# Attention stage of a fused attention, MLP and expert kernel: row sums kept in two DRAM rows, two small PSUM uses moved into the output's banks, scores issued in another order

## The chip, the cores and the metric

The kernel runs on one core of one Trainium2 chip. The metric is device microseconds (us) of one execution; lower is better. Engines are written as in the profile: PE (TensorE, with PEld for its weight loads), DVE (VectorE), ACT (ScalarE), POOL (GpSimd) and SP (SyncE, which here only issues DMAs; "SPq" in the rows). Each engine takes its instructions in order.

## The reference

Block-causal softmax attention, then a leaky MLP, then eight experts mixed by a Sinkhorn-normalised gate. Only the first of the three matters here:

```python
# q, k, v: (4 batches, 8 heads, 576 positions, 64 features), float32
scores = scale * np.matmul(q, k.transpose(0, 1, 3, 2))
scores = np.where(block_i >= block_j, scores, -1000000000.0)   # blocks of 64 positions: 9 x 9
scores = scores - np.max(scores, axis=-1, keepdims=True)
attn = np.exp(scores)
attn = attn / (np.sum(attn, axis=-1, keepdims=True) + 1e-09)
x = np.matmul(attn, v)          # -> (2304 tokens, 512) for the MLP
x = leaky(x @ w_in) @ w_out     # the MLP: 512 -> 2048 -> 512
out = sum_e P[:, e] * (relu(x @ w1[e]) @ w2[e])   # 8 experts, P from 8 rounds of row and column normalisation
```

## The kernel before

The attention works on 16 *pairs*: two heads of one batch, one head on partitions 0 to 63 and one on 64 to 127. A pair's 576 positions are 9 blocks of 64 queries (`NQ = 9`). For a pair p:

- `load_qk` and `load_v` issue its loads on SP: two for q, one for the 64-position tails of q, the same for k, and four for v. `turn_q`, `turn_k` and `turn_tail` transpose q, k and the two tails on PE into a PSUM tile of the pool `ps_tr` (two tiles in turn); ACT copies q out with the scale (`spread`), DVE copies k (`place_k`).
- `scores(p, i, ...)` multiplies query block i with the keys up to it, takes the negated maximum on DVE (`nmax`) and the exponential with its sum on ACT (`ex`, `ssum`). For odd blocks the two heads are written crosswise (`crossed`), so their transposition by `swap` puts them right again.
- `turn_attn(p, g)`, g = 0 to 6, transposes the 25 squares of the exponentials on PE, four at a time (the last one alone), and ACT (g even) or DVE (g odd) copies them into `at`.
- `weigh` multiplies `at` with v into the PSUM tile `av` of the pool `ps_av` (two banks, one tile): `first_product` is the first key chunk, `other_parts` are six products of the other three chunks.
- `totals(p)` forms the reciprocal of the sums, `rsum` (128 partitions x 9), and writes it to a DRAM row of 2 x 576 numbers: one DMA for the five straight (even) blocks of both heads, and one each for the four crossed blocks of either head. `spread_totals(p)` reads that row back with two DMAs, each of which puts one head's 576 numbers on 64 partitions (`by_feature`).
- `split_x(p)` multiplies `av` by `by_feature` on DVE (`xs`) and splits the result into two parts for the MLP (ACT, POOL).

The loop over p overlaps four pairs. The list `turns` sets the order on PE by hand (PE is in `manual_schedule`); "prv", "cur", "nxt" and "fol" in it are the pairs p - 1, p, p + 1 and p + 2. So in *period* p, PE does the scores of pair p + 1, the transpositions and first product of pair p, the other products of pair p - 1 and the turns of pair p + 2. `totals(p)` stands at the period's head, and `load_qk(p + 3)` behind its end. The order on the other engines comes from the framework's scheduler. On SP a period is: three writes of the row, four loads of v, two reads of the row, six loads of q, tails and k; in eight periods a 512 KB load of MLP weights (`wraw`) stands somewhere between. A read of the row waits on SP for the row's writes, and everything behind it on SP waits with it.

Once the attention is done, the MLP and the experts run to the end on PE.

Of the kernel before, what the change touches and what calls it, by code (L numbers as in the profile page):

```python
# [8 lines left out]
F32 = mybir.dt.float32  # L9
# [3 lines left out]
ALU = mybir.AluOpType  # L13
AX = mybir.AxisListType

P = 128
BLK = 64
# [10 lines left out]
def f32(ap):  # L28
    return ap.bitcast(F32)
# [7 lines left out]
def block_attention_mlp_moe(  # L37
# [15 lines left out]
    nc = tc.nc  # L53
    B, H, S, D = q.shape
# [3 lines left out]
    NQ = S // BLK  # L58
# [23 lines left out]
    dram = ctx.enter_context(tc.tile_pool(name="dram", bufs=2, space=bass.MemoryType.DRAM))  # L82
# [10 lines left out]
    def x_parts(c, t0, t1):  # L93

        if t0 < XCUT:
            return [t[:, c, t0:t1] for t in x_first]
        return [t[:, c, t0 - XCUT:t1 - XCUT] for t in x_late]
# [117 lines left out]
    def attention(att, ps_sc, ps_tr, ps_av):  # L215
# [14 lines left out]
        nmax = [att.tile([P, NQ + 1], F32, name=f"nmax{i}") for i in range(2)]  # L230
        ssum = [att.tile([P, NQ + 1], F32, name=f"ssum{i}") for i in range(2)]
        rsum = [att.tile([P, NQ], F32, name=f"rsum{i}") for i in range(2)]
        by_feature = [att.tile([P, S], F32, name=f"by_feature{i}") for i in range(2)]
        xs = att.tile([P, S], F32, name="xs")
        order = [(i, c) for c in range(NKC) for i in range(2 * c, NQ)]
        base = [order.index((2 * c, c)) for c in range(NKC)]
# [38 lines left out]
        def spread(p, src, lo, n):  # L275
            scale = 1.0 / float(D) ** 0.5
            nc.scalar.activation(
                out=qT[p % 2][:, lo * BLK:(lo + n) * BLK], in_=src[:, 0:n * BLK], func=AF.Copy, scale=scale
            )

        def place_k(p, src, lo, hi):
            nc.vector.tensor_copy(out=kT[p % 2][:, lo:hi], in_=src)

        def turn_q(p):
            qm = ps_tr.tile([P, 512], F32, name="qm", tag="tr")
            for t in range(NFULL):
                nc.tensor.transpose(qm[:, t * P:(t + 1) * P], qraw[:, t, :], ident)
            spread(p, qm, 0, W // BLK)
# [5 lines left out]
            place_k(p, km[:, 0:W], 0, W)  # L294

        def turn_tail(p):
            tail = ps_tr.tile([P, 512], F32, name="qk_tail", tag="tr")
            nc.tensor.transpose(tail[:, 0:2 * TAIL], tails, ident)
            spread(p, tail, W // BLK, TAIL // BLK)
            place_k(p, tail[:, TAIL:2 * TAIL], W, S)  # L300
# [41 lines left out]
        rows = {}  # L342

        def totals(p):
            r, s = rsum[p % 2], ssum[p % 2][:, 0:NQ]
            nc.gpsimd.tensor_scalar(out=r, in0=s, scalar1=EPS, scalar2=None, op0=ALU.add)
            nc.vector.reciprocal(out=r, in_=r)
            rows[p] = dram.tile([2, BLK * NQ], F32, name="row", tag="row")
            to = rows[p].rearrange("h (q i) -> h q i", i=NQ)
            nc.sync.dma_start(  # L350
                out=rows[p].rearrange("h (q i) -> (h q) i", i=NQ)[:, 0:NQ:2], in_=r[:, 0:NQ:2]
            )
            for h in range(2):
                nc.sync.dma_start(out=to[1 - h, :, 1:NQ:2], in_=r[h * BLK:(h + 1) * BLK, 1:NQ:2])

        def spread_totals(p):
            with ExitStack() as queued:
                queued.enter_context(tc.issue_after(getattr(fetched[0], "ins", fetched[0])))
                for h in range(2):
                    nc.sync.dma_start(  # L360
                        out=by_feature[p % 2][h * D:(h + 1) * D, :], in_=rows[p][h:h + 1, :].to_broadcast([D, S])
                    )

        def turn_attn(p, g):
            todo = order[4 * g:4 * g + 4]
            n = len(todo)
            tr = ps_tr.tile([P, 4, 2, BLK], F32, name="tr", tag="tr")
            for s, (i, c) in enumerate(todo):
                nc.tensor.transpose(  # L369
                    tr[:, s].rearrange("p h q -> p (h q)"),  # L370
                    ex[p % 2][:, off[i] + c * P:off[i] + (c + 1) * P],
                    swap if i in crossed else ident,
                )
            dst = at[:, 4 * g:4 * g + n]
            if g % 2 == 0:
                nc.scalar.copy(out=dst, in_=tr[:, 0:n])
            else:
                nc.vector.tensor_copy(out=dst, in_=tr[:, 0:n])

        av = {}  # L380

        o = 512 - P

        def weigh(p, c, h, part):
            if (c, h, part) == (0, 0, 0):
                av[p] = ps_av.tile([P, 1024], F32, name="av", tag="av")
            a = at[:, base[c]:base[c] + NQ - 2 * c, h, :]
            r = slice(h * D, (h + 1) * D)
            lhsT = vraw[p % 2][:, c, r]
            if part == 0:  # L390
                nc.tensor.matmul(av[p][r, o:512], lhsT, a[:, 0:2, :], start=True, stop=True)
            else:
                q0 = 2 if c == 0 else 0
                nc.tensor.matmul(  # L394
                    av[p][r, 512 + P * max(c - 1, 0):512 + S - P], lhsT, a[:, q0:, :],
                    start=c == 0, stop=c == NKC - 1,
                )

        def split_x(p):
            b, hp = divmod(p, NPAIR)  # L400
            t = av.pop(p)
            nc.vector.tensor_tensor(  # L402
                out=xs.rearrange("p (i q) -> p i q", q=BLK), in0=t[:, o:o + S].rearrange("p (i q) -> p i q", q=BLK),
                in1=by_feature[p % 2].rearrange("p (q i) -> p i q", i=NQ), op=ALU.mult,
            )
            t0, t1 = b * S, (b + 1) * S
            cuts = [t0, XCUT, t1] if t0 < XCUT < t1 else [t0, t1]
            for u0, u1 in zip(cuts, cuts[1:]):
                hi, lo = x_parts(hp, u0, u1)
                y = xs[:, u0 - t0:u1 - t0]  # L410
                nc.scalar.copy(out=hi, in_=y)
                nc.gpsimd.tensor_tensor(out=lo, in0=y, in1=f32(hi), op=ALU.subtract)
# [3 lines left out]


        first_part = [(weigh, 0, h, part) for part in range(2) for h in range(2)]
        other_parts = [("prv", weigh, c, h, 1) for c in range(1, NKC) for h in range(2)]
        def first_product(p):  # L420
            for f, *a in first_part:
                f(p, *a)

        turns = [
            ("nxt", scores, 8), *other_parts, ("prv", split_x),
            ("nxt", scores, 7, 6), ("cur", turn_attn, 0), ("nxt", load_v), ("fol", turn_q),
            ("nxt", scores, 1, 0), ("cur", turn_attn, 1), ("cur", turn_attn, 2),
            ("nxt", scores, 5, 4), ("fol", turn_tail), ("cur", first_product),
            ("nxt", scores, 3, 2), ("cur", turn_attn, 3), ("fol", turn_k), ("cur", turn_attn, 4),
            ("cur", spread_totals), ("cur", turn_attn, 5), ("cur", turn_attn, 6),  # L430
        ]
        opening = [
            ("nxt", scores, 1, 0), ("nxt", scores, 3, 2), ("nxt", scores, 5, 4), ("nxt", scores, 8),
            ("fol", turn_q), ("nxt", scores, 7, 6), ("nxt", load_v), ("fol", turn_k), ("fol", turn_tail),
        ]

# [11 lines left out]
        for t in vraw:  # L448
            nc.gpsimd.tensor_copy(out=t[TAIL:, NFULL, :], in_=nought[TAIL:, :])
        turn_q(0)  # L450
        turn_k(0)
        turn_tail(0)
        warm(ps_sc, "sc", 3)
        load_qk(1)
# [3 lines left out]
        for p in range(-1, NP + 1):  # L458
            who = {"prv": p - 1, "cur": p, "nxt": p + 1, "fol": p + 2}
            if 0 <= p < NP:  # L460
                totals(p)
            if p == NP:
                first_product(p - 1)
            for w, f, *a in (turns if p >= 0 else opening):
                if 0 <= who[w] < NP and (f is not first_product or p < NP - 1):
                    f(who[w], *a)
                if f is scores and p >= 0 and steps:
                    with ExitStack() as queued:
                        if p + 1 < NP:
                            queued.enter_context(tc.issue_after(getattr(latest[0], "ins", latest[0])))  # L470
                        steps.pop(0)()
            if p + 3 < NP:
                load_qk(p + 3)
# [50 lines left out]
    with (  # L524
        tc.tile_pool(name="att", bufs=1) as att,
        tc.tile_pool(name="ps_sc", bufs=4, space=bass.MemoryType.PSUM) as ps_sc,
        tc.tile_pool(name="ps_tr", bufs=2, space=bass.MemoryType.PSUM) as ps_tr,
        tc.tile_pool(name="ps_av", bufs=1, space=bass.MemoryType.PSUM) as ps_av,
    ):
        with tc.manual_schedule(engines={mybir.EngineType.PE}):  # L530
            attention(att, ps_sc, ps_tr, ps_av)
# [299 lines left out]
    bank, part, hq = {}, {}, {}  # L831
# [377 lines left out]
    for n in range(0, NGR, 2):  # L1209
        p, e, i = groups[n]  # L1210
# [135 lines left out]
```

## Time and profile before

| | us |
|---|---|
| median of 3 runs (2122.15 to 2124.04) | 2122.96 |
| the profiled execution's own time | 2127.02 |
| its span, first to last instruction | 2125.2 |
| PE busy in the span | 2064.7 (97%) |
| DVE / ACT / POOL busy | 1566.6 / 818.6 / 653.7 |
| mean granted TensorE clock | 0.989 |
| first matmul of the MLP starts, from the span's start | 259.0 |
| first write of a row of sums, last one | 17.69, 260.01 |

The attention is the first eighth of the span. In the page's 40 slices of 53 us, PE stands at 7 or 8 tenths in the first five and at 9 (90% or more) in nearly all others. The line numbers below are those of the kernel before: L320 scores, L326 maxima, L333 exponentials, L369 transpositions of the exponentials, L376 and L378 their copies, L391 and L394 products with v, L402 `xs`, L350 and L354 the writes of the row, L360 its reads, L261, L265, L245 and L249 the loads.

### The profile page before, as it was taken

Reading aid. Unit: us, or ns where it says so; the run is one execution under the profiler, and the core shown is the slowest. Engines: PE = TensorE matmul, PEld = TensorE weight load, DVE = VectorE, ACT = ScalarE, POOL = GpSimd, SP = SyncE. Lnnn points to the kernel's source line nnn. Section 1 sums busy time; section 2 is a strip of 40 time slices with the busy share of each in tenths; the row PEclk is TensorE's granted clock in tenths of the full one; section 3 lists DMA queues with packets and bytes.
Section 4 is the critical chain, followed back from the end, with each engine's and each line's share of the span. In section 5 each row is a group of like instructions: output and inputs, shape, how many; then the busy total and the mean of one; then the engine's idle time right before and its main releaser. Section 6 shows DMA issues by size and latency. Waiting matters only on the chain.

```text
span 2125.2 us, 32293 instructions
## 1 busy us (share of the span) xinstructions
PE 2064.7 (97%) x11498; PEld 1853.2 (87%) x11498; DVE 1566.6 (74%) x2671; ACT 818.6 (39%) x1795; POOL 653.7 (31%) x639
## 2 busy tenths in 40 slices
PE   7877799999999999999999999999999999999999
PEld 4444479898888889898989999999999999999998
DVE  6665565656555887887787688888888688888886
ACT  5555433222233454454444333332233423332322
POOL 1121122212202445544543223333232322333322
PEclk9999999999999999999999999999999999999999
DMA  5344311111005888888989777777777777777773
GB/s 116 78 91 97 73 36 50 40 41 50 30 10 189 317 284 310 305 291 297 324 303 339 279 251 262 268 257 265 259 247 274 265 251 252 256 275 254 270 254 111
DMA packets 252642, 436.92 MB, mean 206 GB/s; under 512 B 94761, under 2 KB 131625, under 8 KB 252225
## 3 DMA queue, kind: packets, MB, share of 16 engines
q1 hardware_dynamic: 251280, 434.56, 60.2%
q8 instruction: 91, 1.49, 0.3%
q14 instruction: 71, 0.57, 0.1%
q10 hardware_dynamic: 1200, 0.30, 0.1%
HBM read 308.82 MB, written 125.95 MB: 205 GB/s over the span
## 4 chain that ended last, share of the span: by engine, by line
PE 88%; DMA 6%; DVE 3%; ACT 1%; POOL 1%; SPq 1%; issue 1%; DVEq 0%; ACTq 0%; POOLq 0%
PE h_ps L841 28%; PE o L1009 21%; PE o L1065 12%; PE h_ps L500 9%; PE o L520 9%; DMA row<-rsum 3%; PE o L841 3%; PE sc L320 1%; DMA by_feature<-row 1%; PE tr L369 1%; PE av L394 1%; DMA kraw<-in_k_dram 1%; DVE xs L402 0%; DVE nmax L326 0%; DMA k_0h<-th 0%
## 5 line engine op out<-in xcount | busy, mean ns | idle before, releaser
L938 DVE TENSOR_TENSOR xa<-o,xa 128x384 f32<-128x384 f32 x392 | 216.4, 553 | 111.1 <-PE o L1009 106.9
L841 PE MATMUL h_ps<-xhS,w1h 128*128 128x384 f32 x768 | 257.5, 335 | 0.0
L841 PE MATMUL h_ps<-xhS,w1l 128*128 128x384 f32 x768 | 256.6, 334 | 0.0
L841 PE MATMUL h_ps<-xlS,w1h 128*128 128x384 f32 x768 | 256.6, 334 | 0.0
L938 POOL TENSOR_TENSOR xa<-xa 128x384 f32<-128x384 f32 x92 | 106.1, 1153 | 408.3 <-DVE xa L938 371.1
L938 ACT COPY places<-h_ps 128x384 f32<-128x384 f32 x192 | 92.3, 481 | 287.5 <-PE h_ps L841 219.8
L938 ACT CAST xllate<-xa 128x384 fp32r<-128x384 f32 x120 | 61.8, 515 | 279.3 <-POOL xa L938 279.3
L841 PE MATMUL h_ps<-xhA,w1h 128*128 128x384 f32 x448 | 151.0, 337 | 1.3 <-DVE c L858 1.2
L841 PE MATMUL h_ps<-xhA,w1l 128*128 128x384 f32 x448 | 150.0, 335 | 0.0
L841 PE MATMUL h_ps<-xlA,w1h 128*128 128x384 f32 x448 | 149.9, 335 | 0.0
L841 PEld LDWEIGHTS h_ps<-xhS,w1h 128*128 128x128 f32 x768 | 144.2, 188 | 0.7 <-issue 0.6
L841 PEld LDWEIGHTS h_ps<-xlS,w1h 128*128 128x128 f32 x768 | 144.2, 188 | 0.0
L841 PEld LDWEIGHTS h_ps<-xhS,w1l 128*128 128x128 f32 x768 | 144.1, 188 | 0.0
L1065 PE MATMUL o<-w2h,xhlate 128*128 128x512 f32 x408 | 143.8, 391 | 0.0
L938 POOL TENSOR_TENSOR places<-places 128x384 f32<-128x384 f32 x60 | 60.8, 1014 | 251.1 <-DVE wa L938 234.4
L1065 PE MATMUL o<-w2h,xllate 128*128 128x512 f32 x384 | 133.9, 389 | 0.0
L1009 PE MATMUL o<-xllate,w2h 128*128 128x384 f32 x480 | 122.8, 336 | 0.0
L755 POOL TENSOR_TENSOR wa<-wraw 128x256 f32<-128x256 f32 x32 | 29.8, 931 | 300.6 <-DVE w1l L773 269.1
L1009 PE MATMUL o<-xhlate,w2h 128*128 128x384 f32 x480 | 121.8, 334 | 0.0
L520 PE MATMUL o<-hh,w2h 128*128 128x512 f32 (+1 forms) x320 | 117.8, 369 | 0.0
L520 PE MATMUL o<-hh,w2l 128*128 128x512 f32 (+1 forms) x320 | 117.7, 368 | 0.0
L508 DVE TENSOR_TENSOR g<-h_ps,g 128x512 f32<-128x512 f32 (+1 forms) x80 | 50.9, 636 | 87.8 <-ACT g L507 87.6
(254 smaller groups left out, 5722.3 us busy)
## 6 DMA issues: line engine op xcount, KB each, us to landing
wraw<-in_moe_w_dram SPq DMA_DIRECT2D x64, 512.0 KB, 3.6
w1h<-k_1h SPq DMA_DIRECT2D x64, 512.0 KB, 4.7
w1l<-k_1l SPq DMA_DIRECT2D x64, 512.0 KB, 6.6
w2h<-k_1h SPq DMA_DIRECT2D x60, 512.0 KB, 5.9
w2l<-k_1l SPq DMA_DIRECT2D x60, 512.0 KB, 6.4
w1h<-k_0h SPq DMA_DIRECT2D x64, 384.0 KB, 4.2
w1l<-k_0l SPq DMA_DIRECT2D x64, 384.0 KB, 4.4
w2h<-k_0h SPq DMA_DIRECT2D x60, 384.0 KB, 4.4
```

What stands on the lines that cost most here:

```text
L320: nc.tensor.matmul(sc[o:o + BLK, :], qT[p % 2][r, i * BLK:(i + 1) * BLK], kT[p % 2][r, lo:hi], start=True, stop=True,)
L369: nc.tensor.transpose(tr[:, s].rearrange("p h q -> p (h q)"), ex[p % 2][:, off[i] + c * P:off[i] + (c + 1) * P], swap if i in crossed else ...
L394: nc.tensor.matmul(av[p][r, 512 + P * max(c - 1, 0):512 + S - P], lhsT, a[:, q0:, :], start=c == 0, stop=c == NKC - 1,)
L500: nc.tensor.matmul(ps[:, 0:n], w[:, c, cols], x, start=c == 0 and s == 0, stop=c == KC - 1 and s == 2,)
L508: nc.vector.tensor_tensor(out=g[:, 0:n], in0=ps[:, 0:n], in1=g[:, 0:n], op=ALU.max)
L520: nc.tensor.matmul(ps[:, 0:n], w[:, cut], h[:, 0:n], start=start and m == 0, stop=stop and m == 2)
L755: nc.gpsimd.tensor_tensor(out=one[:, 0], in0=a21, in1=a22, op=ALU.add)
L841: mm = nc.tensor.matmul(ps, w[:, c], x[:, c], start=first and c == 0 and s == 0, stop=c == 1 and s == 2, skip_group_check=True,)
L938: ins = f(*a, **k)
L1009: mm = nc.tensor.matmul(o, a, b, start=i == 0, stop=i == 5)
L1065: mm = nc.tensor.matmul(o, h, w, start=m == 0, stop=m == 11)
```

## The change

The diff, cut to its core:

```diff
-        by_feature = [att.tile([P, S], F32, ...) for i in range(2)]
+        NPAR = ((NQ + 1) // 2, NQ // 2)
+        by_feature = [[att.tile([P, BLK * n], F32, ...) for n in NPAR] for i in range(2)]
...
+        def av_tile(p):
+            if p not in av:
+                av[p] = ps_av.tile([P, 1024], F32, name="av", tag="av")
+            return av[p]
...
         def turn_tail(p):
-            tail = ps_tr.tile([P, 512], F32, name="qk_tail", tag="tr")
+            if 0 <= p - 2:
+                tail = av_tile(p - 2)
+            else:
+                tail = ps_tr.tile([P, 512], F32, name="qk_tail", tag="tr")
...
-            rows[p] = dram.tile([2, BLK * NQ], F32, name="row", tag="row")
-            to = rows[p].rearrange("h (q i) -> h q i", i=NQ)
-            nc.sync.dma_start(
-                out=rows[p].rearrange("h (q i) -> (h q) i", i=NQ)[:, 0:NQ:2], in_=r[:, 0:NQ:2]
-            )
-            for h in range(2):
-                nc.sync.dma_start(out=to[1 - h, :, 1:NQ:2], in_=r[h * BLK:(h + 1) * BLK, 1:NQ:2])
+            rows[p] = []
+            for c, n in enumerate(NPAR):
+                t = dram.tile([2, BLK * n], F32, name=f"row{c}", tag=f"row{c}")
+                nc.sync.dma_start(out=t.rearrange("h (q i) -> (h q) i", i=n), in_=r[:, c:NQ:2])
+                rows[p].append(t)
...
                 for h in range(2):
-                    nc.sync.dma_start(out=by_feature[p % 2][h * D:(h + 1) * D, :], in_=rows[p][h:h + 1, :]...)
+                    for c, t in enumerate(rows[p]):
+                        g, n = (1 - h if c else h), BLK * NPAR[c]
+                        nc.sync.dma_start(out=by_feature[p % 2][c][h * D:(h + 1) * D, :], in_=t[g:g + 1, :]...)
...
+            if n == 1:
+                tr = av_tile(p)[:, P:2 * P].rearrange("p (s h q) -> p s h q", s=1, h=2)
+            else:
+                tr = ps_tr.tile([P, 4, 2, BLK], F32, name="tr", tag="tr")
...
-            nc.vector.tensor_tensor(out=xs..., in0=t..., in1=by_feature[p % 2]..., op=ALU.mult)
+            for c, n in enumerate(NPAR):
+                nc.vector.tensor_tensor(out=xs...[:, c:NQ:2], in0=t...[:, c:NQ:2], in1=by_feature[p % 2][c]..., op=ALU.mult)
...
         turns = [
-            ("nxt", scores, 8), *other_parts, ("prv", split_x),
-            ("nxt", scores, 7, 6), ("cur", turn_attn, 0), ("nxt", load_v), ("fol", turn_q),
-            ("nxt", scores, 1, 0), ("cur", turn_attn, 1), ("cur", turn_attn, 2),
-            ("nxt", scores, 5, 4), ("fol", turn_tail), ("cur", first_product),
-            ("nxt", scores, 3, 2), ("cur", turn_attn, 3), ("fol", turn_k), ("cur", turn_attn, 4),
+            ("nxt", scores, 8), ("cur", turn_attn, 0), *other_parts[0:2],
+            ("nxt", scores, 3, 2), *other_parts[2:], ("prv", split_x), ("nxt", load_v), ("cur", turn_attn, 1),
+            ("nxt", scores, 5, 4), ("cur", turn_attn, 2), ("fol", turn_q),
+            ("nxt", scores, 1, 0), ("fol", turn_tail), ("cur", first_product), ("cur", turn_attn, 3),
+            ("nxt", scores, 7, 6), ("fol", turn_k), ("cur", turn_attn, 4),
             ("cur", spread_totals), ("cur", turn_attn, 5), ("cur", turn_attn, 6),
         ]
```

The sums go to two DRAM tiles, one for the five straight blocks and one for the four crossed ones, with one write each and two reads each; the crossing is done by the reads. `split_x` becomes two multiplications. The tails of pair p + 2 are transposed into the `av` tile of pair p, in the bank that later also holds the first part of pair p's product, and so is the last, single transposition of `turn_attn`. The list `turns` has a new order.

On SP, one loop of a steady period, before. `rsum` is the source of the row, `vraw`, `qraw`, `tails`, `kraw` are the loads, and x2 means two in a row:

```order
L360 DMA by_feature_121<-row 64x576 x2
L261 DMA qraw<-in_q_dram 128x4x64 x2
L265 DMA tails<-in_q_dram 64x2x64
L265 DMA tails<-in_k_dram 64x2x64
L141 DMA wraw<-in_moe_w_out_dram 128x1024
L261 DMA kraw<-in_k_dram 128x4x64 x2
L350 DMA row<-rsum_120 128x5x1
L354 DMA row<-rsum_120 64x4x1 x2
L245 DMA vraw_106<-in_v_dram 128x4x64
L249 DMA vraw_106<-in_v_dram 64x64
```

and the same piece of SP now:

```order
L371 DMA by_feature_123<-row_1313 64x320
L371 DMA by_feature_124<-row_1315 64x256
L371 DMA by_feature_123<-row_1313 64x320
L371 DMA by_feature_124<-row_1315 64x256
L262 DMA qraw<-in_q_dram 128x4x64 x2
L266 DMA tails<-in_q_dram 64x2x64
L266 DMA tails<-in_k_dram 64x2x64
L262 DMA kraw<-in_k_dram 128x4x64 x2
L362 DMA row_1463<-rsum_119 640x1x1
L362 DMA row_1465<-rsum_119 512x1x1
L246 DMA vraw_107<-in_v_dram 128x4x64
L250 DMA vraw_107<-in_v_dram 64x64
```

The order of the kinds is the same; two reads have become four and three writes two. A write's shape (128x5x1, 640x1x1) is in elements of one number on both sides.

On PE, the head of a period before, up to the instructions behind `other_parts` (the 64x448 to 64x64 products), with `sc` for scores:

```order
L320 MATMUL sc<-kT_111,qT_108 64x288 x4
L394 MATMUL av<-at,vraw_106 64x448 x2
L394 MATMUL av<-at,vraw_106 64x320 x2
L394 MATMUL av<-at,vraw_106 64x192 x2
L394 MATMUL av<-at,vraw_106 64x64 x2
L320 MATMUL sc<-kT_111,qT_108 64x512 x2
L320 MATMUL sc<-kT_111,qT_108 64x448 x2
```

and now:

```order
L331 MATMUL sc<-kT_111,qT_108 64x288 x4
L383 MATMUL tr<-ident,ex_114 128x128
L383 MATMUL tr<-swap,ex_114 128x128
L383 MATMUL tr<-ident,ex_114 128x128
L383 MATMUL tr<-swap,ex_114 128x128
L405 MATMUL av<-at,vraw_106 64x448 x2
L331 MATMUL sc<-kT_111,qT_108 64x256 x2
L331 MATMUL sc<-kT_111,qT_108 64x192 x2
L405 MATMUL av<-at,vraw_106 64x320 x2
L405 MATMUL av<-at,vraw_106 64x192 x2
L405 MATMUL av<-at,vraw_106 64x64 x2
```

A group of transpositions and the scores of blocks 3 and 2 have moved ahead of the last product, on which `split_x` waits.

On PE, the turn of the tails and the first product before, with the semaphores that an instruction waits for:

```order
L320 MATMUL sc<-kT_111,qT_108 64x320 x2
L298 MATMUL qk_tail<-ident,tails 128x128 [waits DMAHW3_49,DMAHW2_49,DVE_49]
L391 MATMUL av<-at,vraw_107 64x128
L391 MATMUL av<-at,vraw_107 64x128 [waits DMAHW4_49]
L394 MATMUL av<-at,vraw_107 64x448 [waits Activation_49]
L394 MATMUL av<-at,vraw_107 64x448
```

and now:

```order
L331 MATMUL sc<-kT_111,qT_108 64x64 [waits Activation_49]
L331 MATMUL sc<-kT_111,qT_108 64x64
L309 MATMUL av<-ident,tails 128x128 [waits DMAHW6_49,DMAHW5_49]
L402 MATMUL av<-at,vraw_107 64x128 [waits DVE_49]
L402 MATMUL av<-at,vraw_107 64x128
L405 MATMUL av<-at,vraw_107 64x448 x2
```

The first product of pair p now stands behind a wait for DVE: the copy of k's tail out of the same bank, which itself stands behind ACT's copy of q's tail.

## Rows read from the trace of the kernel before

**Rows 1.** Busy time by stretch: PE, PEld, DVE, ACT, POOL, granted clock, DMA share, GB/s

```profile
180.00:220.00 40.00, 31.01 (x236) 16.52 (x238) 24.86 (x52) 22.49 (x74) 11.76 (x14) 0.91 0.42 80
259.00:300.00 41.00, 41.00 (x210) 31.71 (x211) 19.10 (x27) 11.60 (x22) 6.56 (x7) 1.00 0.08 17
```

**Rows 2.** What SP waited for, 40 to 262 us: total, times, longest

```profile
SPq L360 <- DMA row<-rsum: 82.7, 18, 9.0
```

**Rows 3.** SP's issues in order of time: start, length, line, DMA, count

```profile
164.03 0.80 SPq L350 DMA_DIRECT2D row<-rsum  x1
164.87 1.27 SPq L354 DMA_DIRECT2D row<-rsum  x2
...
174.34 1.09 SPq L360 DMA_DIRECT2D by_feature<-row  x2
175.48 1.13 SPq L261 DMA_DIRECT2D qraw<-in_q_dram  x2
...
179.30 0.45 SPq L350 DMA_DIRECT2D row<-rsum  x1
...
192.92 0.45 SPq L141 DMA_DIRECT2D wraw<-in_moe_w_out_dram  x1
```

**Rows 4.** SP's issues at the stage's start and its end

```profile
17.69 0.55 SPq L350 DMA_DIRECT2D row<-rsum  x1
...
26.99 1.12 SPq L360 DMA_DIRECT2D by_feature<-row  x2
...
244.21 1.53 SPq L360 DMA_DIRECT2D by_feature<-row  x2
...
260.01 0.37 SPq L350 DMA_DIRECT2D row<-rsum  x1
```

**Rows 5.** Chain that ended last, 160 to 192 us: start, length, what

```profile
165.53 8.73 DMA row<-rsum
...
174.84 4.08 DMA by_feature<-row
...
179.05 1.19 DVE xs L402
```

**Rows 6.** The same chain from 14 to 262 us, its longest landing of a row

```profile
130.49 12.14 DMA row<-rsum
```

**Rows 7.** DMA issues: count, KB each, median us to landing

```profile
by_feature<-row SPq DMA_DIRECT2D x32, 144.0 KB, 3.7
...
vraw<-in_v_dram SPq DMA_DIRECT2D x32, 128.0 KB, 9.6
...
row<-rsum SPq DMA_DIRECT2D x32, 1.0 KB, 8.8
```

**Rows 8.** PE in order of time, a period from its scores 8 to the next

```profile
209.64 1.20 PE L320 MATMUL sc<-kT,qT 64*64 64x288 f32 x8
...
216.00 0.33 PE L369 MATMUL tr<-ident,ex 128*128 128x128 f32 x1 [0.88 <-ACT at L376]
...
217.11 0.44 PE L369 MATMUL tr<-ident,ex 128*128 128x128 f32 x2 [0.46 <-ACT qT L277]
...
222.24 0.33 PE L369 MATMUL tr<-ident,ex 128*128 128x128 f32 x1 [0.70 <-DVE wa L154]
...
223.89 1.19 PE L320 MATMUL sc<-kT,qT 64*64 64x288 f32 x8
```

**Rows 9.** PE in order of time, the last disturbed period

```profile
252.35 0.69 PE L369 MATMUL tr<-ident,ex 128*128 128x128 f32 x2 [3.94 <-ACT at L376]
...
253.40 1.54 PE L320 MATMUL sc<-kT,qT 64*64 64x384 f32 x8
...
256.99 0.88 PE L320 MATMUL sc<-kT,qT 64*64 64x256 f32 x8
```

**Rows 10.** Groups of DVE and ACT, 14 to 262 us: busy, mean ns, idle before

```profile
L378 DVE COPY at<-tr 128x512 f32<-128x512 f32 x44 | 30.2, 687 | 11.2 <-PE tr L369 10.4 <-issue 0.6
L402 DVE TENSOR_TENSOR xs<-av,by_feature 128x576 f32<-128x576 f32 x14 | 16.6, 1187 | 32.8 <-DMA by_feature<-row 24.9 <-PE av L394 6.7 <-DMA kraw<-in_k_dram 1.3
...
L282 DVE COPY kT<-qk_tail 128x64 f32<-128x64 f32 x14 | 3.1, 224 | 5.3 <-ACT qT L277 4.6
...
L277 ACT ACTIVATE qT<-qm 128x512 f32<-128x512 f32 x14 | 8.5, 604 | 0.0
...
L277 ACT ACTIVATE qT<-qk_tail 128x64 f32<-128x64 f32 x14 | 3.0, 215 | 2.1 <-PE qk_tail L298 2.1
```

More of the change, by code (lines that the diff above doesn't have):

```diff
@@ L232, in attention @@
         rsum = [att.tile([P, NQ], F32, name=f"rsum{i}") for i in range(2)]
-        by_feature = [att.tile([P, S], F32, name=f"by_feature{i}") for i in range(2)]
+        NPAR = ((NQ + 1) // 2, NQ // 2)
+        by_feature = [[att.tile([P, BLK * n], F32, name=f"by_feature{i}{n}") for n in NPAR] for i in range(2)]
         xs = att.tile([P, S], F32, name="xs")
@@ L282, in place_k @@
             nc.vector.tensor_copy(out=kT[p % 2][:, lo:hi], in_=src)
+        av = {}
+        def av_tile(p):
+            if p not in av:
+                av[p] = ps_av.tile([P, 1024], F32, name="av", tag="av")
+            return av[p]
         def turn_q(p):
@@ L359, in spread_totals @@
                 for h in range(2):
-                    nc.sync.dma_start(
-                        out=by_feature[p % 2][h * D:(h + 1) * D, :], in_=rows[p][h:h + 1, :].to_broadcast([D, S])
-                    )
+                    for c, t in enumerate(rows[p]):
+                        g, n = (1 - h if c else h), BLK * NPAR[c]
+                        nc.sync.dma_start(
+                            out=by_feature[p % 2][c][h * D:(h + 1) * D, :], in_=t[g:g + 1, :].to_broadcast([D, n])
+                        )
         def turn_attn(p, g):
@@ L366, in turn_attn @@
             n = len(todo)
-            tr = ps_tr.tile([P, 4, 2, BLK], F32, name="tr", tag="tr")
+            if n == 1:
+                tr = av_tile(p)[:, P:2 * P].rearrange("p (s h q) -> p s h q", s=1, h=2)
+            else:
+                tr = ps_tr.tile([P, 4, 2, BLK], F32, name="tr", tag="tr")
             for s, (i, c) in enumerate(todo):
@@ L378, in turn_attn @@
                 nc.vector.tensor_copy(out=dst, in_=tr[:, 0:n])
-        av = {}
         o = 512 - P
         def weigh(p, c, h, part):
-            if (c, h, part) == (0, 0, 0):
-                av[p] = ps_av.tile([P, 1024], F32, name="av", tag="av")
+            av_tile(p)
             a = at[:, base[c]:base[c] + NQ - 2 * c, h, :]
@@ L401, in split_x @@
             t = av.pop(p)
[L402 to L405, printed above, removed]
+            for c, n in enumerate(NPAR):
+                nc.vector.tensor_tensor(
+                    out=xs.rearrange("p (i q) -> p i q", q=BLK)[:, c:NQ:2],
+                    in0=t[:, o:o + S].rearrange("p (i q) -> p i q", q=BLK)[:, c:NQ:2],
+                    in1=by_feature[p % 2][c].rearrange("p (q i) -> p i q", i=n), op=ALU.mult,
+                )
             t0, t1 = b * S, (b + 1) * S
```

## The prediction

> **What bounds the kernel now.** I read the busy times by stretch first. From 259 us on PE is busy without a gap at a granted clock of 1.00, the upper level of 2.4 GHz; in the attention it works 31.01 of 40 us at 0.91 [rows 1]. Behind the attention the program is the same on both sides, so what the change moves at 259 us moves the end by as much. The question is only what sets the attention's pace.
>
> Next the waits of SP's queue. SP stood 82.7 us at L360, the read of the row, 18 times, waiting for the row's writes [rows 2]. Its issues show the loop [rows 3]. The row is issued from 164.03 on, the reads at 174.34, 10.31 later; then come two reads, six loads, and the next row at 179.30, 4.96 later, with nothing waited for between. So this loop takes 15.27 us. The first row is issued at 17.69 and the sixteenth at 260.01 [rows 4], fifteen loops of 242.32 / 15 = 16.15 on average.
>
> The chain of waits says that this loop is a bound: last write of the row 8.73, read 4.08, then `xs` [rows 5], with landings up to 12.14 in other periods [rows 6]. Over all issues the row's median is 8.8 us for a thousand bytes, while a read of 144 KB takes 3.7 [rows 7]. PE in order of time shows its own need: in a stretch where it is hardly held up, a period lasts 209.64 to 223.89 = 14.25 us, waits of 0.88 + 0.46 + 0.70 = 2.04 included [rows 8]. PE could go 1.9 us faster per period than the loop on SP lets it. A disturbed period looks otherwise: PE stands 3.94 us behind an `at` copy [rows 9], because DVE is held at `xs` by the late read (24.9 us idle ahead of `xs` for by_feature, [rows 10]) and the copies stand behind it.
>
> So the change is to be priced on SP's loop first, and on PE only as far as PE's period would pass 16.15.
>
> **Four reads instead of two.** Two reads take 175.48 - 174.34 = 1.14 us of SP, 0.57 each [rows 3]. Two more cost 1.14 per loop. But the first read of each head now waits for the straight row alone, which is issued first and should land first; the second waits for the crossed row. If the first read goes out before the crossed row has landed, one of the two extra issues lies in the wait. Bounds: +0.57 and +1.14 per loop. I take +0.57, since the straight row is more than half of the elements and goes first. Fourteen groups of reads stand between 26.99 and 244.21 [rows 4]: 14 x 0.57 = +8.0 us.
>
> **Two writes of the row instead of three.** The number of elements is the same, 5 x 128 + 4 x 128 = 1152, and each is still written by itself, as the order's shapes say (640x1x1 and 512x1x1): the source takes every second of nine numbers. Before, the second of the two L354 writes was issued at about 165.5 and the chain counts 8.73 from there. If the landing is set by the last issue, one issue less gives 1.27 / 2 = 0.64 us. If it is set by the drain of 1152 elements, which begins with the first issue, it gives nothing. Bounds 0 and -0.64 for the issue; I take -0.4, nearer to the first end, since the rows count 8.73 and the median of 8.8 from an issue on, and the last issue is what goes. 14 x -0.4 = -5.6. Whether two dense rows (20 and 16 bytes in a piece) take elements faster than one row in which each write skips every second place, the trace doesn't show: no write there is dense. The forecast takes the landing as it is; half of the spread seen (8.73 to 12.14), 1.7 either way, goes to the rivals below.
>
> Beside it the Trainium skill has a rule, in "DMA: Bandwidth & Descriptors", section "Rules for kernel authors": a transfer whose last dimension isn't contiguous falls apart into a descriptor per element. By it the strided source alone keeps the landing where it is, and the sum without any gain on the writes would be 2128 (the second rival's lower end). The trace agrees as far as it goes, with 8.8 us for 1 KB against 3.7 for 144 KB [rows 7].
>
> **One load of MLP weights less in the loop.** `wraw` takes 0.45 us of SP [rows 3]. In the order it stands between the reads and the next row in six loops before and in five now: -0.5.
>
> **PE's new order.** A group of transpositions and the scores of blocks 3 and 2 move ahead of the last product, on which `split_x` waits; so `xs` can start later by these. As `xs` waited 24.9 us for by_feature and only 6.7 for PE [rows 10], most of this is cover that exists. The old waits of PE for ACT and DVE copies (0.88, 0.46 and 0.70) should mostly go, as the turns are pulled apart. In their place comes one: the first product stands behind DVE's copy of k's tail, which stands behind ACT's copy of q's. Its bounds are the two copies alone, 0.215 + 0.224 = 0.44 [rows 10], and the copies with what ACT has ahead of them, the spread of q at 604 ns twice, some 1.2, and a hand-over, near 2 in all. Between 2.04 removed and 0.44 to 2 added, PE's own period comes to 12.7 to 14.2. Queued behind that wait are only PE's own next scores. All of it lies within SP's loop of 16.15, so I count 0.
>
> **`xs` in two operations.** It took 1187 ns for 576 columns, 2.06 ns a column against 687 / 512 = 1.34 for a copy [rows 10]. Two halves of 320 and 256 columns cost between -0.4 (at the copy's rate: 576 x 1.34 = 772) and +0.1 (one more start). DVE's `xs` isn't on SP's loop, since the next row is issued without waiting for it: 0.
>
> **The end.** The last `split_x` ahead of 259 us has less PE work behind it than before: the scores of 1.54 and 0.88 and some transpositions [rows 9] are done earlier. Bounds 0 and -3, taken -2, since PE idles then anyway while the last read lands.
>
> **Sum.** +8.0 - 5.6 - 0.5 - 2 = -0.1, that is nothing. Against the profile's own time of 2127.02 (span 2125.2 and 1.8 around it) this is 2127; the three runs have 2122.96 as median, so that the profiled execution is 4.06 above them, and I put the difference on the median: **2123 us**. What a measurement of this kernel can tell from no change is 0.2%, 4.2 us: 2118.7 to 2127.2. The forecast's own range, from the bounds of these terms without a change in the landing's size, is 2117 to 2128.
>
> **Rivals.**
>
> *The row lands earlier, and the loop falls until PE's own period is the bound (faster).* For it: a row with its own dense place, written in one piece in the order of partitions, against crossed writes that come a second and third time to the same places; straight and crossed no longer share a stretch. Against it: the same 1152 elements. A saving of 0.7 us per loop on top gives 14 x 0.7 = 10, 2113; from a saving of 2 us on, the loop is at PE's 14.2, (16.15 - 14.2) x 14 + 2.5 = 30, 2093. Middle: 1.2 us, 17 + 2.5 + what PE's clock gives back as it idles less, about 2100.
>
> *The row lands no earlier, and the four reads are paid in full (slower).* The place is L360's wait on SP; the price is +0.57 per loop with the landing unchanged: 14 x 0.57 - 2.5 = +5.5, 2128. If the second landing comes later as well, because the two rows and the loads of v (9.6 us median, [rows 7]) share the same queue in another order, half of the spread from 8.73 to 12.14 is 1.7: 14 x (0.57 + 1.7) - 2.5 = +29, 2152. It decides as soon as the landing saves less than 0.1 us per loop. For it: nothing in the trace shows a gain for fewer writes of the same elements. Against it: half of the reads can go while the crossed row is still on its way.
>
> *PE becomes the bound.* If the first product's wait comes to 2 us and the old waits stay, PE's period is 16.2, equal to the loop now: +1 x 14 at most with the clock at 0.91, 2137. The waits in rows 8 were for copies that are now given more room, so I hold it unlikely, and count it with the slower case.
>
> *The change doesn't do what it says.* The rows are two, but their writes stay one element each; then the count of DMAs changes and the time doesn't: that is the forecast.
>
> **How the numbers follow.** Forecast 0.40, of which 0.06 fall below 2118.7, 0.26 within 0.2%, 0.08 above. First rival 0.34, all faster. Second, with the third, 0.26, all slower. Faster by over 0.2%: 0.06 + 0.34 = 0.40. Within: 0.26. Slower: 0.08 + 0.26 = 0.34. The range reaches to the deep end of the first rival (2093) and nearly to the end of the second (2150). As it holds both signs, the forecast's own 2117 to 2128 stands beside it.
>
> **What would show it.** In SP's issues the first row to the first read should shrink from 10.31 to about 8 or less, while the first row to the second read stays near 10; four reads with pitch 0.57, and the next row some 5.5 after the second read. Fifteen loops from the first row to the last should still be about 242. If the time from the row's issue to the last landing drops by a microsecond or more, the first rival is right; if L360's wait grows above 82.7, the second. On PE I look for a wait ahead of the first product, by DVE's kT copy, of 0.4 to 2 us, and for the 0.88, 0.46 and 0.70 to be gone. `xs` should show about 660 and 530 ns. A first MLP matmul more than 5 us away from 259 would make the forecast wrong.

## The result, and the profile after

| | before | changed |
|---|---|---|
| median, us (runs) | 2123.5 (4) | 2149.88 (4, 2145.83 to 2153.86) |
| ratio, 95% interval | | 1.012, 1.0089 to 1.015 |
| the profiled execution, us | 2127.02 | 2146.18 |
| first matmul of the MLP, us from the span's start | 259.0 | 282.45 |

The change made the kernel 1.2% slower. The time was lost in the attention: the MLP's first matmul starts 23 us later, the profiled execution ends 19 us later.

Busy times by stretch of the changed kernel (PE, PEld, DVE, ACT, POOL, granted clock, DMA share, GB/s), the answer to [rows 1]:

```profile
180.00:220.00 40.00, 30.61 (x196) 15.31 (x196) 20.04 (x45) 17.24 (x60) 7.25 (x10) 0.79 0.45 77
259.00:300.00 41.00, 36.10 (x215) 22.84 (x212) 20.65 (x39) 16.81 (x43) 4.80 (x6) 0.91 0.35 48
```

In the first stretch PE did 196 matmuls where it had done 236, and DVE 45 operations where it had done 52. The granted clock fell from 0.91 to 0.79: PE stood more, and what it did took longer too. This stretch is the worst one. Over the six stretches from 20 to 259 us PE did 1285 matmuls in 182.56 us of busy time where it had done 1412 in 189.99, at a clock of 0.79 to 0.91 where it had been 0.91 in five stretches and 0.87 in one.

What SP waited for in the changed kernel from 40 to 262 us (total, times, longest), the answer to [rows 2]:

```profile
SPq L371 <- DMA row<-rsum: 85.1, 17, 8.1
```

SP's issues in order of time, one loop of the changed kernel from a row's first write to the next (start, length, line, DMA, count), and below the first and last row, the answers to [rows 3, 4]:

```profile
177.80 1.25 SPq L362 DMA_DIRECT2D row<-rsum  x2
179.15 1.20 SPq L246 DMA_DIRECT2D vraw<-in_v_dram  x1
...
189.39 3.00 SPq L371 DMA_DIRECT2D by_feature<-row  x4
192.49 1.08 SPq L262 DMA_DIRECT2D qraw<-in_q_dram  x2
...
195.08 1.10 SPq L262 DMA_DIRECT2D kraw<-in_k_dram  x2
196.28 1.26 SPq L362 DMA_DIRECT2D row<-rsum  x2
```

```profile
17.14 1.26 SPq L362 DMA_DIRECT2D row<-rsum  x2
...
285.35 1.25 SPq L362 DMA_DIRECT2D row<-rsum  x2
```

From the row to the first read it is 11.59 us in this loop, and the four reads take 3.00 where two had taken 1.09. Fifteen loops take 268.21 us, 17.88 each, against 16.15. The table below has the three stretches of a loop (row to first read, reads, rest) as means over thirteen loops, worked out from such rows of every kernel. By these means the first and the last stretch are as before.

DMA issues of the changed kernel (KB each, median us from issue to landing), the answer to [rows 7]:

```profile
vraw<-in_v_dram SPq DMA_DIRECT2D x32, 128.0 KB, 10.2
by_feature<-row SPq DMA_DIRECT2D x32, 80.0 KB, 3.4
by_feature<-row SPq DMA_DIRECT2D x32, 64.0 KB, 3.1
...
row<-rsum SPq DMA_DIRECT2D x16, 2.5 KB, 10.8
row<-rsum SPq DMA_DIRECT2D x16, 2.0 KB, 11.8
```

The straight row of 640 numbers lands 10.8 us after its issue, only one microsecond sooner than the crossed one. So the first read, which waits for the straight row alone, goes out no earlier than before.

PE's waits in order of time in the changed kernel, the answer to [rows 8]:

```profile
196.43 0.66 PE L295 MATMUL qm<-ident,qraw 128*128 128x128 f32 x4 [2.53 <-DVE at L392]
199.45 0.70 PE L402 MATMUL av<-at,vraw 128*64 128x128 f32 x4 [1.74 <-DVE kT L283]
206.78 1.09 PE L301 MATMUL km<-ident,kraw 128*128 128x128 f32 x4 [2.18 <-DMA kraw<-in_k_dram]
```

The new wait of the first product is there (1.74), beside waits that come from SP's late loads and from DVE. DVE's groups from 14 to 285 us (busy, mean ns, idle before), the answer to [rows 10]:

```profile
L414 DVE TENSOR_TENSOR xs<-av,by_feature 128x320 f32<-128x320 f32 x14 | 10.2, 729 | 16.2 <-DMA by_feature<-row 11.3 <-ACT ex L344 2.3 <-PE tr L383 2.1
L414 DVE TENSOR_TENSOR xs<-av,by_feature 128x256 f32<-128x256 f32 x14 | 8.4, 602 | 0.9 <-DMA by_feature<-row 0.7
L283 DVE COPY kT<-av 128x64 f32<-128x64 f32 x14 | 3.1, 224 | 8.8 <-ACT qT L278 8.7
```

The two multiplications cost 729 + 602 = 1331 ns, 144 more than the one of before.

### The profile page after: what moved, and what is told of

Its sections match the earlier page's. It is cut to its first block, busy times and chain, and to the rows that moved or that the text cites. A ratio compares the mean times of both kernels' runs of the same rounds, so it can differ in the third digit from the quotient of the medians.

```text
span 2144.4 us, 32404 instructions
## 1 busy us (share of the span) xinstructions
PE 2073.6 (97%) x11498; PEld 1853.6 (86%) x11498; DVE 1561.2 (73%) x2687; ACT 816.5 (38%) x1795; POOL 654.3 (31%) x639
## 4 chain that ended last, share of the span: by engine, by line
PE 87%; DMA 5%; DVE 4%; ACT 1%; issue 1%; SPq 1%; POOL 0%; DVEq 0%; ACTq 0%; POOLq 0%
PE h_ps L854 28%; PE o L1022 20%; PE o L1078 12%; PE o L533 9%; PE h_ps L513 9%; PE o L854 3%; DMA row<-rsum 2%; PE sc L331 2%; DMA kraw<-in_k_dram 1%; PE tr L383 1%; PE av L405 1%; DMA by_feature<-row 1%; DVE nmax L337 1%; DMA wraw<-in_moe_w_out_dram 1%; DVE xa L951 0%
## 5 line engine op out<-in xcount | busy, mean ns | idle before, releaser
L951 POOL TENSOR_TENSOR xa<-xa 128x384 f32<-128x384 f32 x92 | 106.0, 1152 | 408.1 <-DVE xa L951 370.8
```

What stands on the lines that cost most here:

```text
L951: ins = f(*a, **k)
```

## The experiments

Theory A: the reads lengthen SP's loop, and the loop sets the attention's pace. Rival B: PE's new order, with the first product's wait, does. Of theory A's cause, two more: C, a row's landing is the time of 1152 single elements; D, it is set by the loads of v beside it. The ratio is to the kernel before, timed beside them on the same chip: 2124.75 us for e1 to e4, 2124.84 for e5 to e8, 2126.24 for e9 to e12. The middle columns are means in us over thirteen loops from the first row on, from SP's issues.

| kernel | median | ratio, 95% interval | row to first read | reads | rest | loop |
|---|---|---|---|---|---|---|
| before | | | 10.78 | 1.40 | 4.32 | 16.48 |
| changed | 2149.88 | 1.012 (1.0089 to 1.015) | 10.81 | 3.18 | 4.32 | 18.31 |
| e1 rows only | 2143.46 | 1.0087 (1.0069 to 1.0104) | 10.82 | 2.95 | 4.28 | 18.04 |
| e2 order only | 2124.53 | 0.9996 (0.9984 to 1.0007) | 10.64 | 1.38 | 4.41 | 16.43 |
| e3 two dense rows | 2121.04 | 0.9981 (0.9971 to 0.9992) | 6.46 | 2.53 | 7.13 | 16.12 |
| e4 dense, two reads | 2121.45 | 0.9982 (0.9971 to 0.9994) | 6.47 | 1.19 | 8.21 | 15.88 |
| e5 dense, old order | 2089.89 | 0.9832 (0.9818 to 0.9845) | 6.07 | 1.21 | 6.44 | 13.72 |
| e6 dense, tail in own tile | 2088.12 | 0.9827 (0.9813 to 0.9842) | 6.44 | 1.16 | 5.92 | 13.53 |
| e7 two dense rows, old order | 2090.85 | 0.9839 (0.9824 to 0.9854) | 5.80 | 2.71 | 5.22 | 13.74 |
| e8 dense, product later | 2074.25 | 0.976 (0.9747 to 0.9774) | 6.55 | 1.17 | 4.92 | 12.64 |
| e9 changed, product later | 2148.24 | 1.0106 (1.009 to 1.0122) | 10.64 | 3.48 | 4.26 | 18.39 |
| e10 old rows, product later | 2125.83 | 0.9996 (0.9986 to 1.0007) | 10.70 | 1.29 | 4.42 | 16.41 |
| e11 four reads only | 2143.24 | 1.008 (1.0066 to 1.0095) | 10.74 | 2.88 | 4.17 | 17.81 |
| e12 dense source, row as before | 2125.43 | 0.9996 (0.9986 to 1.0007) | 10.96 | 1.14 | 4.76 | 16.86 |

**Rows or order.** e1 has the rows, reads and multiplications of the change, in the order and the banks of before; e2 has the order and the banks of the change, with the row of before.

```diff
 # e1, against the changed kernel
-        turns = [... new order ...]
+        turns = [... order of before ...]
-            if 0 <= p - 2:
-                tail = av_tile(p - 2)
+            tail = ps_tr.tile([P, 512], F32, name="qk_tail", tag="tr")
 # e2, against the changed kernel
-            for c, n in enumerate(NPAR): ... two DRAM tiles, two writes, four reads, two multiplications
+            rows[p] = dram.tile([2, BLK * NQ], F32, name="row", tag="row")   # three writes, two reads, one
```

> The kernel before with the two DRAM rows alone (two writes, four reads, two multiplications in split_x); the order of turns and the banks stay as before. Theory A (the four reads lengthen SP's loop: 1.40 to 3.18 us from the first read's issue to the last one's end, over 15 loops): the whole loss is here, 2123.5 + 15 x 1.8 = 2150, between 2142 and 2158, with that stretch of the loop again near 3.2. Rival B (PE's new order and the wait at the first product): no loss here, 2119 to 2128.

> The kernel before with the new order of turns and the two uses moved into the output's banks; the row and its three writes and two reads stay as before. Theory A: SP's loop stays at 16.2 to 16.5 us, and the time at 2117 to 2127, less what the shorter end gives. Rival B: the loss is here, 2140 to 2155, and the wait of PE for DVE's copy of k's tail is what PE stands in, over 2 us per period.

Measured: e1 is 0.87% slower with reads of 2.95 us, e2 shows no change. A holds, B falls. The intervals of e1 and of the changed kernel overlap, so that a small share of the order in the loss is neither shown nor excluded; the loops are 18.04 and 18.31 us long.

**The reads alone.** e11 splits each read of the kernel before into halves; nothing else differs.

```diff
-                    nc.sync.dma_start(out=by_feature[p % 2][h * D:(h + 1) * D, :], in_=rows[p][h:h + 1, :]...)
+                    for c in (slice(0, S // 2), slice(S // 2, S)):
+                        nc.sync.dma_start(out=by_feature[p % 2][h * D:(h + 1) * D, c], in_=rows[p][h:h + 1, c]...)
```

> The kernel before, but each read of the row in two halves of 288 numbers: three writes, one row, four reads, all behind the same landing. Theory A (issues are what the reads cost): first read's issue to the last one's end grows from 1.40 to about 2.5 us, 15 x 1.14 = 17 us, 2135 to 2145. If the loss came from the two rows or their landing instead: 2120 to 2130.

Measured: 2143.24, 0.8% slower, practically the loss of e1, with one row and one multiplication. The reads take 2.88 us per loop, 1.48 more than before. Four reads that go out undisturbed take 2.37 us, against 1.09 for two, so the two issues cost 1.28. The rest comes from single issues that take 1.1 to 2.3 us in place of 0.6, in five of the first thirteen loops (2.91 for four in the second row shown); why they do stays open. SP's issues of this kernel:

```profile
112.77 2.37 SPq L361 DMA_DIRECT2D by_feature<-row  x4
...
130.68 2.91 SPq L361 DMA_DIRECT2D by_feature<-row  x4
```

**What the landing is made of.** e3 and e4 put the sums straight first and crossed behind, by the column into which each exponential accumulates, so that a write has 20 or 16 bytes in one piece. e3 keeps two rows and four reads; e4 has one row, three writes and two reads.

```diff
-                        bias=x, scale=1.0, accum_out=sm[:, i + s:i + s + 1],
+                        bias=x, scale=1.0, accum_out=sm[:, NQ if s else at_col(i):][:, 0:1],
 # at_col(i) = i // 2 + (i % 2) * 5
 # e3
-                nc.sync.dma_start(out=t.rearrange("h (q i) -> (h q) i", i=n), in_=r[:, c:NQ:2])
+                nc.sync.dma_start(out=t.rearrange("h (q i) -> (h q) i", i=n), in_=r[:, c * NPAR[0]:][:, 0:n])
 # e4: one row, blocks of a query in the order 0 2 4 6 8 1 3 5 7
+            nc.sync.dma_start(out=rows[p].rearrange("h (q i) -> (h q) i", i=NQ)[:, 0:5], in_=r[:, 0:5])
+                nc.sync.dma_start(out=to[1 - h, :, 5:NQ], in_=r[h * BLK:(h + 1) * BLK, 5:NQ])   # h = 0, 1
```

> The changed kernel, but the sums are kept straight ones first and crossed ones behind (the exponentials' sums are accumulated into these places), so that the source of each write is dense: 20 or 16 bytes in one piece, 256 pieces instead of 1152. Two writes and four reads as in the changed kernel. Theory C (the landing is the time of 1152 single elements): row to first read falls from 10.8 us to 4 to 6, the loop to under 14, PE becomes the bound, 2085 to 2105. Rival D (the landing is set by the loads of v beside it in the same queue): row to first read stays above 9.5 and the time within 2143 to 2155.

> The changed kernel's order and banks, the dense source, but one DRAM row again with three writes (each 128 or 64 pieces of 20 or 16 bytes) and two reads. Theories A and C together: the loop on SP is shorter than in the kernel with two dense rows by about 1.1 us of reads less 0.6 for the third write, but PE is the bound in both, so the two are within 8 us of each other, 2080 to 2105. Rival D: row to first read above 9.5, time as with order only, 2117 to 2127.

DMA issues of e3, as above:

```profile
vraw<-in_v_dram SPq DMA_DIRECT2D x32, 128.0 KB, 2.4
by_feature<-row SPq DMA_DIRECT2D x32, 80.0 KB, 2.7
by_feature<-row SPq DMA_DIRECT2D x32, 64.0 KB, 2.6
...
row<-rsum SPq DMA_DIRECT2D x16, 2.5 KB, 1.9
row<-rsum SPq DMA_DIRECT2D x16, 2.0 KB, 2.4
```

The rows land in 1.9 and 2.4 us in place of 10.8 and 11.8, and the loads of v, issued behind them, in 2.4 in place of 10.2. C holds, and D had it the wrong way round: the elements of the row held up the loads. But the time lies only 0.2% under the kernel before, where some 20 us or more were expected. The loops are still 16.12 and 15.88 us long. SP hardly waits for the row any more, and stands for PE in its place, as its waits in e4 from 40 to 262 us show:

```profile
SPq L262 <- PE km L301: 37.2, 12, 4.0
SPq L246 <- PE av L408: 32.5, 12, 3.2
...
SPq L374 <- DMA row<-rsum: 0.5, 1, 0.5
```

PE's waits in e4 from 40 to 240 us, and its order of time over one period from its scores 8:

```profile
PE av L405 <- DVE kT L283: 22.8, 12, 2.6
PE tr L386 <- DVE kT L283: 14.2, 12, 1.5
```

```profile
124.82 1.19 PE L334 MATMUL sc<-kT,qT 64*64 64x288 f32 x8
...
134.26 0.44 PE L405 MATMUL av<-at,vraw 128*64 128x128 f32 x4 [1.74 <-DVE kT L283]
...
140.89 0.44 PE L386 MATMUL tr<-ident,ex 128*128 128x128 f32 x2 [1.24 <-DVE kT L283]
...
141.59 1.19 PE L334 MATMUL sc<-kT,qT 64*64 64x288 f32 x8
```

Two waits for DVE's copies of k, 22.8 / 12 = 1.9 and 1.2 us per period, come with the new order and its banks. With them PE needs some 16 us per period, nearly what SP's old loop took. That is how e2 could show no loss: one bound lay under the other.

e12 is the reverse test, on e8 below: a dense source, but the row in the order of before, so that each number again goes to a place of its own.

```diff
-                out=rows[p].rearrange("h (q i) -> (h q) i", i=NQ)[:, 0:m], in_=r[:, 0:m]
+                out=rows[p].rearrange("h (q i) -> (h q) i", i=NQ)[:, 0:NQ:2], in_=r[:, 0:m]
...
-                nc.sync.dma_start(out=to[1 - h, :, m:NQ], in_=r[h * BLK:(h + 1) * BLK, m:NQ])
+                nc.sync.dma_start(out=to[1 - h, :, 1:NQ:2], in_=r[h * BLK:(h + 1) * BLK, m:NQ])
```

> The fastest kernel so far (dense source, three writes, two reads, first product later), but the row in its old order, so that the source is dense and every number goes to its own place two apart: 1152 single elements again. Theory C (the number of pieces sets the landing, whichever side makes them): landing about 9 to 10 us again, SP's wait back, 2112 to 2128. Rival (the strided source is what is slow): landing near 2 us, 2070 to 2080.

Measured: 2125.43, the time of the kernel before, 51 us above e8, and SP waits again: the row to the first read takes 10.96 us. The DMA queue's packets in e12 and in e8, and SP's wait in e12 from 40 to 262 us:

```profile
q1 hardware_dynamic: 251280, 434.56, 60.7%
```

```profile
q1 hardware_dynamic: 236944, 434.56, 61.1%
```

```profile
SPq L374 <- DMA row<-rsum: 74.8, 17, 8.2
```

The bytes are the same; the packets differ by 14336 = 16 pairs x (1152 - 256). So one strided side is enough to make single elements, and with them SP's wait for the landing is back.

**PE's order, with SP's loop out of the way.** e5 and e7 have the dense writes with the order and the banks of before (e5 as e4, e7 as e3); e6 is e4 with the tails' transposition in its own tile; e8 is e4 with the first product two steps later.

```diff
 # e6
-            if 0 <= p - 2:
-                tail = av_tile(p - 2)
+            tail = ps_tr.tile([P, 512], F32, name="qk_tail", tag="tr")
 # e8
-            ("nxt", scores, 1, 0), ("fol", turn_tail), ("cur", first_product), ("cur", turn_attn, 3),
-            ("nxt", scores, 7, 6), ("fol", turn_k), ("cur", turn_attn, 4),
+            ("nxt", scores, 1, 0), ("fol", turn_tail), ("cur", turn_attn, 3),
+            ("nxt", scores, 7, 6), ("cur", first_product), ("fol", turn_k), ("cur", turn_attn, 4),
```

> Dense source, one DRAM row, three writes and two reads, with the order of turns and the banks of the kernel before. With the dense source SP waits no more for the row, so that the time shows PE's own period in this order. Theory E (the new order's period is about 16 us by itself, from its waits for DVE's copies of k, 1.9 and 1.2 us per period; the old order's is 14.25): 14 x 1.75 = 24 us under the two dense kernels with the new order, 2093 to 2106. Rival F (something common to both orders, as DVE's and ACT's own work, makes a period of 16): 2116 to 2126, as with the new order.

> Two dense rows, two writes and four reads as in the changed kernel, with the order of turns and the banks before. It tells what four reads cost once SP has slack: by theory A (their price is a price of SP's loop only) within 4 us of the dense kernel with two reads in the same order; if reads cost by themselves (more packets, later by_feature), 8 us or more above it.

> Dense source, three writes, two reads, the new order of turns, the last single transposition in the output's bank, but the tails' transposition in its own tile as in the kernel before, so that the first product needs no copy of k's tail to be done. Theory E1 (this wait, 1.9 us per period, is the price of the bank): 14 x 1.9 = 27 at most, 2095 to 2110, and the wait of PE for DVE at the first product gone. Rival: the wait moves to the next transposition that needs a tile of that pool (which has two), 2116 to 2126.

> Dense source, three writes, two reads, the banks of the changed kernel, and its order with the first product two steps later (behind the fourth group of transpositions and the scores of blocks 7 and 6). Theory E1: DVE's copy of k's tail is done by then, the wait of 1.9 us goes, 2095 to 2112. Rival: DVE is late at that point anyway, and PE waits for the same DVE queue at the next copy: 2116 to 2126.

Measured: e5 2089.89 and e7 2090.85, so two reads more cost nothing that can be seen once SP has slack, and the order and banks of before have the shorter period (13.72 against 15.88 in e4). e6 takes the wait at the first product away, and with it 33 us: in the new order, too, the period is 13.53. So it is not the order by itself that makes e4 slow, but the tails' turn in the output's bank with the first product right behind it. The second wait for DVE's copy of k stays in e6 (14.9 / 12 = 1.2). Both e5 and e6 came out under what was expected. PE's waits in e6 from 40 to 210 us:

```profile
PE tr L383 <- DVE kT L283: 14.9, 12, 1.5
PE qk_tail L306 <- ACT at L390: 7.5, 12, 0.6
```

e8 keeps the bank and only gives the copies time. It is the fastest, 2074.25, under all that was expected. Its PE waits from 40 to 210 us:

```profile
PE tr L386 <- ACT at L393: 4.3, 12, 0.4
PE tr L386 <- DVE kT L283: 4.2, 12, 0.4
PE av L405 <- DVE kT L283: 3.3, 4, 1.2
```

The stretch from 100 to 140 us in e4, e6 and e8, one row each (columns as above):

```profile
100.00:140.00 40.00, 32.77 (x224) 15.68 (x224) 22.12 (x49) 17.89 (x60) 6.23 (x8) 0.87 0.34 83
```

```profile
100.00:140.00 40.00, 34.28 (x280) 18.18 (x276) 30.79 (x65) 24.18 (x78) 10.43 (x12) 1.00 0.46 116
```

```profile
100.00:140.00 40.00, 36.47 (x298) 18.92 (x296) 29.77 (x66) 25.16 (x83) 9.67 (x13) 1.00 0.46 114
```

In e8 PE does 298 matmuls in 40 us at the full granted clock, in e4 224 at 0.87. A matmul took 32.77 / 224 = 0.146 us of busy time in e4 and 34.28 / 280 = 0.122 in e6. So the waits that went gave the clock back too, and more than their own length. In order of time the periods of e8 are 12.9 us:

```profile
129.29 0.44 PE L386 MATMUL tr<-ident,ex 128*128 128x128 f32 x2 [0.35 <-DVE kT L283]
...
142.20 0.44 PE L386 MATMUL tr<-ident,ex 128*128 128x128 f32 x2 [0.35 <-DVE kT L283]
...
155.13 0.44 PE L386 MATMUL tr<-ident,ex 128*128 128x128 f32 x2 [0.35 <-DVE kT L283]
```

**The same move under SP's loop.** e9 and e10 make e8's move of the first product in the changed kernel and in e2, with single elements.

> The changed kernel (two rows, single elements, four reads) with the first product two steps later. With dense rows that move was worth 47 us. Theory A (with single elements SP's loop of 18.3 us sets the pace, so PE's waits are cover): no gain, 2140 to 2154. Rival B (PE's wait at the first product had its own share of the loss): 2095 to 2130.

> The row, its three writes and two reads of the kernel before, with the new order, the banks, and the first product two steps later. Theory A: SP's loop of 16.4 us sets the pace as before, 2114 to 2126. Rival (PE's period of 16 us in the new order was the bound beside it, and half of the move comes through): 2085 to 2108.

Measured: 2148.24 and 2125.83, no gain from either. A move that is worth 47 us with dense rows (e4 to e8) is worth nothing while SP's loop is longer than PE's period.

## Why the prediction was right or wrong

The range held the time (2149.88 in 2093 to 2150) by 0.1 us, and that was luck in the size. The forecast of no change was wrong. The second rival named the right place, the reads on SP's queue behind a row that lands no earlier, and the signs came that had been set for it and against the forecast: SP's wait for the row grew from 82.7 to 85.1, and the MLP's first matmul moved by 23 us. But its upper price, 2152, is +0.57 for the reads and +1.7 for a later second landing, and not what was paid. Its lower price doesn't fit its name: four reads "paid in full" are two extra issues, by the prediction's own bound +1.14 and not +0.57, so 14 x 1.14 - 2.5 = +13, 2137.

- *SP's loop is the bound*: right, in before and in the changed kernel (e9, e10 against e8).
- *"I take +0.57, since the straight row is more than half of the elements and goes first"*: this is the step that failed. The straight row lands 10.8 us after its issue, the crossed one 11.8: the two come nearly together, and not one well ahead of the other. The first read moved by 0.03 us (10.78 to 10.81). So no issue lies hidden in the wait, and both extra ones are paid: +1.78 per loop measured (1.40 to 3.18) against +0.57. Of this, 1.28 are the two issues. About 0.5 are the second read's wait for the crossed row: by the single issues of thirteen loops it starts 0.97 us behind the first read, against 0.50 in e11, where all four wait for the same landing.
- *"I take -0.4" for the third write's issue*: wrong, 0. The row to the first read stays at 10.6 to 11.0 in all kernels with single elements, whether two writes make them or three; it is the bound "drain of 1152 elements". The Trainium skill's rule of a descriptor per element ("DMA: Bandwidth & Descriptors", section "Rules for kernel authors"), which spoke against a gain on the writes, agrees with e3 and e12, and with the 14336 packets between e12 and e8.
- *The load of MLP weights, -0.5*: not seen; the rest of the loop is 4.32 us on both sides.
- *The sum by what was measured*: fifteen loops take 268.21 - 242.32 = 25.9 us more, against 26 between the medians and 23 at the MLP's first matmul.
- *PE's new order, 0*: right for the time, wrong in its size. PE's own need in the order of before was read well (14.25, and 13.72 in e5). In the new one the old waits went, but the wait at the first product came near its upper bound (1.74 in the row shown, 1.9 on average in e4), and a second one for DVE's copy of k (1.2) came that the prediction does not have. With the clock lower besides, the period is 16 us and not 12.7 to 14.2. It was hidden, as the third rival has it, "equal to the loop now". With the product later, the period is 12.9.
- *`xs` -0.4 to +0.1*: measured +0.14, just outside, and off the bound, as said.
- *The end, -2*: neither shown nor excluded. The MLP's first matmul starts 2.9 us ahead of the sixteenth row in the changed kernel and 1.0 before, but 5.2 ahead in e1, which has the order of before. In e2, with the new order at the end, the interval leaves room for 3.4 us at most.
- *First rival, an earlier landing by dense rows*: dense places in DRAM alone give nothing (10.81). Source and place have to be dense both.

## What to carry to other kernels

Where one queue waits in the middle of a loop that sets the pace, a DMA added behind the wait costs its issue in every loop, and splitting a transfer so that a part can be waited for earlier pays only if that part lands earlier, which the landing times of the parts tell. A small transfer that takes longer to land than a hundred times larger one is to be asked for its number of pieces first: here a permutation of nine columns, without an instruction more (e3 against the changed kernel), took the landing from 11 us to 2. And an order of work is to be judged with the other bound taken away: the new one with its banks looked harmless under SP's loop, cost 32 us when the loop was cured (e4 against e5), nearly all of it by one wait, and with one product moved was the best of all.

## What the runs showed of the hardware

The loads of v, 128 KB each, landed in 10.2 us behind 1152 single elements and in 2.4 behind 256 pieces with the same bytes, in one queue. The granted clock in the attention, in five stretches of 40 us from 20 us on, was 0.79 to 0.91 in the changed kernel, 0.87 to 1.00 in e4, and 1.00 throughout in e5 to e8. From e4 to e6 a wait of 1.9 us per period went, 27 us in 14 periods, and the time fell by 33.
